# Hashed attention and a gated layer on one core: the loads of the first heads, the bits of the queries, and the place where the first late set's weights are fetched

## The chip, the core and the metric

The kernel runs on one core of a Trainium2 chip. The core has a matrix engine (PE; its weight loads are shown apart, as PEld), a vector engine (DVE), an activation engine (ACT), a general engine (POOL) and a queue engine that only issues transfers (SP). Each executes its instructions in the order in which they were written, and waits on semaphores for the others. Transfers are issued from SP, and a few from ACT; 16 DMA engines carry them out. The metric is the device time of one execution, in microseconds (us).

## What is computed

Four batches of eight heads, 768 tokens each, 64 numbers per head. A key counts for a query only if the signs of six projections agree; the heads' results, laid side by side, go through a gated layer with 1536 inner columns:

```python
q_bits = (np.einsum('bhsd,dk->bhsk', q, proj) > 0).astype(np.int64)
k_bits = (np.einsum('bhsd,dk->bhsk', k, proj) > 0).astype(np.int64)
...
mask = q_bucket[:, :, :, None] == k_bucket[:, :, None, :]
scores = scale * np.matmul(q, k.transpose(0, 1, 3, 2))
scores = np.where(mask, scores, -1000000000.0)
...
attn = np.exp(scores)
attn = attn / (np.sum(attn, axis=-1, keepdims=True) + 1e-09)
return np.matmul(attn, v).astype(np.float32)
...
gate = 1.0 / (1.0 + np.exp(-(x @ w_gate)))
val = x @ w_val
return (gate * val @ w_out).astype(np.float32)
```

## The kernel before

The work is a list of tasks. Each names an engine, a key, an estimated duration, the tasks that it comes after and the buffers that it takes and gives back. A planner (`Plan.order`) walks through the list in estimated time; on each engine the task with the smallest key that is ready and has its buffers goes next. What it writes down is the fixed order of each engine. So an estimate decides an order, but no duration on the chip.

**The heads.** There are 16 pairs of heads. Of each pair the keys and queries are loaded (kr, qr), turned on PE (tk, tq, L945), copied (kx, qx), and split into a high and a low part (kh, kl, qh, ql) whose three cross products make up a full-precision product. SP copies the queries' parts into the other half of the partitions (qsh, qsl, L974). A product with the projection (hs, L980; its table is hw) gives the signs, DVE makes bits of them (L987), and SP spreads these over two tiles, qb (four transfers, L993) and kb (four, L1002). A score task (sc, L1053 and L1059) is one product of the bits, which pushes unlike pairs apart, and six of the parts. DVE finds the extreme and moves the scores to e (L1069), ACT takes the exponential (L1077), PE turns e (tp, L1110), DVE or ACT copies it to ef (L1117), and PE multiplies with the values (pv, L1127; vr is the loaded v). The sums go by two transfers through memory (rd, rb) to POOL, which divides (xs, L1137); SP stores xs to xd. A pair has 12 score tasks, in two groups of six.

At the start, PE runs 60 matmuls on a tile of zeros whose result nobody reads (idle, L271, the fillers). They have the largest key of all.

**The weights.** They come as 64-bit numbers. Beside the heads, DVE, ACT and POOL convert and split them (L320 to L384). The pieces of the first two blocks of 128 inner columns stay on chip; the others go to memory (kg, kv, ko).

**The early units.** A unit is half of a batch's tokens. It loads xd to xr (L463), casts xh on ACT (L470), subtracts xl on POOL or DVE (L474), and does for the first two blocks two gate products (zg, L500), two value products (zv), a gated product gf (DVE, L516) split into gh and gl (L520, L521), and three output products (zo, L533), copied to ob and stored as part.

**The late sets.** After the heads, the other ten blocks are done in five sets of two, batch by batch, each by seven products (z1 to z7, L719) of sums of four blocks of x (a11, a12, a21, a22, s1 to s4). The blocks are loaded as ra (L617); the sum of two of them, s1, stands in a tile that is named sc like the scores (L625). The weights of a set are ten fetches, four wg, four wv, two wo (L688). They begin with the task `switch`, which closes the pools of the heads' stage and opens the late ones.

## Time and profile before

| | us |
|---|---|
| median of 3 runs | 1017.61 |
| lowest and highest | 1016.65, 1025.71 |
| profiled execution | 1016.87 |
| its span in the trace | 1014.9 |
| PE, DVE, ACT, POOL busy | 979.6, 762.2, 559.9, 288.2 |

The span runs from the first to the last instruction in the trace; the execution's own time has another 2 us around it. The heads end at about 513, the last early unit at about 557; the late sets fill the rest. In the profile's rows an instruction stands with its start, its duration and, in brackets, how long its engine sat idle before it and what ended that. An arrow in a wait reads "waited for". A busy share of PE counts the fillers too.

### The profile page before, as it was taken

The numbers are of one execution on the slowest core, as the hardware profiler recorded it, in microseconds if no ns is written. First come the engines' busy times: TensorE is split into PE (matmuls) and PEld (weight loads), VectorE is DVE, ScalarE is ACT, GpSimd is POOL, SyncE is SP. The second block draws the span as 40 slices with busy tenths as digits, with TensorE's granted clock in tenths as the row PEclk, the third lists the DMA queues.
The fourth block names the chain that finished last, engine by engine and source line by source line (L and its number), as shares of the span: only waits on it lengthen the run. The fifth ranks groups of instructions, "written<-read, shape, count | busy, mean of one in ns | idle before, by whom it ended". The sixth has DMA issues, their size and how long they took to land.

```text
span 1014.9 us, 20971 instructions
## 1 busy us (share of the span) xinstructions
PE 979.6 (97%) x8108; PEld 779.9 (77%) x8108; DVE 762.2 (75%) x1412; ACT 559.9 (55%) x1022; POOL 288.2 (28%) x259
## 2 busy tenths in 40 slices
PE   7999999999999999999979999999999999999998
PEld 3665566676666666675668989999989989999897
DVE  2878997898777778887615787888787778787864
ACT  1778787877677778887644352343233325242430
POOL 4024346555554366463443121211000000000000
PEclk9999999999999999999998999999999999999999
DMA  7355666576775668645467977588359671505021
GB/s 159 90 148 147 168 170 176 183 227 180 219 200 190 183 179 261 184 144 184 167 245 261 383 285 258 203 281 310 140 185 385 210 274 42 187 16 171 32 93 63
DMA packets 145988, 192.43 MB, mean 190 GB/s; under 512 B 65248, under 2 KB 104416, under 8 KB 145888
## 3 DMA queue, kind: packets, MB, share of 16 engines
q1 hardware_dynamic: 144160, 190.69, 58.3%
q8 instruction: 64, 1.05, 0.4%
q10 hardware_dynamic: 1728, 0.40, 0.2%
q14 instruction: 36, 0.29, 0.1%
HBM read 127.41 MB, written 49.28 MB: 174 GB/s over the span
## 4 chain that ended last, share of the span: by engine, by line
PE 78%; DVE 8%; DMA 6%; SPq 3%; ACT 2%; issue 1%; POOL 1%; DVEq 0%; ACTq 0%; POOLq 0%
PE yo L838 16%; PE pv L1127 11%; PE sc L1059 7%; PE tp L1110 5%; PE zo L533 3%; DVE e L1069 3%; PE sc L1053 3%; PE zg L500 3%; DMA rawv<-in_moe_w_val_dram 2%; PE zv L500 2%; PE z4g L719 2%; PE z1g L719 2%; PE z1v L719 2%; PE z4v L719 2%; PE z7v L719 2%; PE z3v L719 2%
## 5 line engine op out<-in xcount | busy, mean ns | idle before, releaser
L1077 ACT ACTIVATE e<-e,st 128x768 f32<-128x768 f32 x192 | 178.6, 932 | 47.8 <-DVE e L1069 47.0
L1069 DVE TENSOR_SCALAR_CACHE_REDUCE e<-sc 128x768 f32<-128x768 f32 x192 | 176.3, 953 | 26.9 <-PE sc L1059 26.0
L1127 PE MATMUL pv<-ef,vr 128*64 128x384 f32 x768 | 143.4, 503 | 0.8 <-DVE ef L1117 0.8
L1110 PEld LDWEIGHTS tp<-ident,e 64*128 64x128 f32 x2304 | 84.6, 139 | 36.5 <-issue 14.7
L1110 PE MATMUL tp<-ident,e 64*128 64x64 f32 x2304 | 95.3, 226 | 7.2 <-DVE e L1069 3.1
L1117 DVE COPY ef<-tp 128x768 f32<-128x768 f32 x88 | 83.0, 950 | 21.5 <-PE tp L1110 21.4
L1117 ACT COPY ef<-tp 128x768 f32<-128x768 f32 x104 | 81.3, 797 | 31.1 <-PE tp L1110 30.5
L1127 PEld LDWEIGHTS pv<-ef,vr 128*64 128x64 f32 x768 | 48.8, 138 | 57.8 <-issue 48.7
L1059 PE MATMUL sc<-kh,ql 64*128 64x384 f32 x192 | 89.8, 468 | 0.0
L1059 PE MATMUL sc<-kh,qsl 64*128 64x384 f32 x192 | 89.8, 468 | 0.0
L1053 PE MATMUL sc<-kb,qb 64*128 64x384 bf16 x384 | 66.1, 330 | 10.4 <-DMA kb<-bits 2.7
L1059 PE MATMUL sc<-kh,qh 64*128 64x384 f32 x192 | 64.3, 335 | 0.0
L1059 PE MATMUL sc<-kh,qsh 64*128 64x384 f32 x192 | 64.2, 335 | 0.0
L1059 PE MATMUL sc<-kl,qh 64*128 64x384 f32 x192 | 64.0, 333 | 0.0
L1059 PE MATMUL sc<-kl,qsh 64*128 64x384 f32 x192 | 64.0, 333 | 0.0
L1053 PEld LDWEIGHTS <-qb 64*128 64x128 bf16 x384 | 22.6, 94 | 49.7 <-issue 41.1
L1137 POOL TENSOR_TENSOR xs<-xs,rb 128x384 f32<-128x384 f32 x32 | 32.7, 1022 | 71.4 <-DVE xs L1134 60.4
L739 ACT COPY snm1g<-z1g 128x384 f32<-128x384 f32 x20 | 9.6, 481 | 76.1 <-PE z1g L719 76.1
L838 PE MATMUL yo<-wo,gh 128*128 128x512 f32 x144 | 44.6, 391 | 0.0
L877 DVE TENSOR_TENSOR ol<-yo,ol 128x512 f32<-128x512 f32 x36 | 24.7, 687 | 23.4 <-PE yo L838 22.8
L500 PE MATMUL zg<-xh,wg 128*128 128x384 f32 x128 | 38.7, 361 | 3.6 <-ACT xh L470 3.6
L1059 PEld LDWEIGHTS sc<-kh,qsl 64*128 64x128 f32 x192 | 37.3, 194 | 1.5 <-issue 1.5
(562 smaller groups left out, 2817.7 us busy)
## 6 DMA issues: line engine op xcount, KB each, us to landing
wg<-kg SPq DMA_DIRECT2D x33, 512.0 KB
wv<-kv SPq DMA_DIRECT2D x33, 512.0 KB
ra<-xd SPq DMA_DIRECT2D x32, 384.0 KB
wo<-ko SPq DMA_DIRECT2D x22, 512.0 KB
part<-ob SPq DMA_DIRECT2D x36, 256.0 KB
kg<-pkg SPq DMA_DIRECT2D x15, 512.0 KB
kv<-pkv SPq DMA_DIRECT2D x15, 512.0 KB
kr<-in_k_dram SPq DMA_DIRECT2D x64, 96.0 KB
```

Of the source, the lines that this page charges most:

```text
L500: nc.tensor.matmul(z["acc"][:, :GN], a[:, wc], x[xx][c // 2][:, c % 2, :], start=(c == 0 and i == 0), stop=(c == KC - 1 and i == 2),)
L533: nc.tensor.matmul(acc, a[:, slot, ts_], w, start=(first and i == 0), stop=(last and i == 2))
L719: nc.tensor.matmul(bank[m], a[:, wc], x[xx, block][:, c, :], start=(c == 0 and i == 0), stop=(c == 1 and i == 2),)
L838: nc.tensor.matmul(accs[t], a[:, ts_], w, start=(start and jj == 0 and q == 0), stop=(stop and jj == 1 and q == 2),)
L1053: nc.tensor.matmul(sc[:, j, :GN], z["qb"][rows, c], z["kb"][rows, h], start=True, stop=False, tile_position=(j * D, 0),)
L1059: nc.tensor.matmul(sc[:, j, :GN], q_[rows, c], z["k" + x][rows, h * GN : (h + 1) * GN], start=False, stop=(m == 2), tile_position=(j * D, 0),)
L1069: nc.vector.tensor_scalar(sp(e), gz["sc", t, h][:, :, :GN], MASKED, None, op0=ALU.min, op1=ALU.min, accum_out=gz["st", t][:, h : h + 1],)
L1077: nc.scalar.activation(e, e, AF.Exp, bias=st[:, h : h + 1], scale=-1.0, accum_out=gz["su"][:, h * GT + t : h * GT + t + 1],)
L1110: nc.tensor.transpose(tp[:, r, at_ : at_ + D], gz["e", t, h][rows, c * P : (c + 1) * P], ident[rows, rows], tile_position=(r * D, 0),)
L1117: copy(gz["ef", c].rearrange("p (n r d) -> p r n d", r=2, d=D), gz["tp", c][:, :, :GN].rearrange("p r (n d) -> p r n d", d=D),)
L1127: nc.tensor.matmul(gz["pv"][rows, :GN], z["v"][:, h, c], gz["ef", c][:, h * GN : (h + 1) * GN], start=(c == 0), stop=(c == NC - 1), tile_p ...
L1137: nc.gpsimd.tensor_mul(gz["xs"], gz["xs"], gz["rb"])
```

## The change

**Start.** The zeros of the fillers have a tile of their own, set by POOL before anything else; before, they were the last of POOL's settings. The table hw is cleared on DVE. A small activation at the head of ACT makes the activation table load there. The projection is loaded ahead of the queries, both from ACT. In the plan, the second pair's loads come after the first pair's have landed, the third pair's after all that the first pair needs, and the first values after the first keys and queries. The low parts of the first pair are left to DVE.

**Bits.** The four row groups of hs are arranged otherwise, so that DVE writes the bits of the queries into qb itself: half of the query columns stand where the scores read them, and two transfers, not four, bring the other half across. For the lower partitions the two halves of qb are then swapped (`beyond`). The keys' bits are spread from qb; for the first pair ACT issues these four transfers.

**Weights and the late stage.** The conversion starts at step 6 of the scores, not 12, with two buffers for raw weights in place of one. The staging tiles and kr, qr, kx, qx lie in a pool on the other side of the memory. When the early weights and the last pair's tiles are done with it, a task `first` closes that pool and opens one for the ten weights of the set that is worked first. `switch` then waits until the last stores of xs have begun, not ended, and the new pools wait tile by tile. The ra loads get a larger key, and a12 is split second. The fetches of the second set wait for the early product that last used their tile, not for the last of all. The planner no longer chooses a filler because its tiling fits.

At the start, SP before and now, from the first row (kr, qr, vr with the pair in the number; the size behind):

```order
L928 DMA kr_0_218<-in_k_dram 128x3x64 x4
L937 DMA vr_0_227<-in_v_dram 128x2x384
L928 DMA kr_1_230<-in_k_dram 128x3x64 x4
L933 DMA qr_1_243<-in_q_dram 128x6x64 x2
L937 DMA vr_1_251<-in_v_dram 128x2x384
L928 DMA kr_2_287<-in_k_dram 128x3x64 x4
L974 DMA qsh_0_311<-qh_0_302 64x768 x2
L933 DMA qr_2_321<-in_q_dram 128x6x64 x2
L993 DMA qb_198<-bits_0_338 24x384 x4
L974 DMA qsl_0_367<-ql_0_303 64x768 x2
L1002 DMA kb_200<-bits_0_338 12x384 x4
```

```order
L941 DMA kr_0_225<-in_k_dram 128x3x64 x4
L950 DMA vr_0_262<-in_v_dram 128x2x384
L941 DMA kr_1_277<-in_k_dram 128x3x64 x4
L946 DMA qr_1_302<-in_q_dram 128x6x64 x2
L987 DMA qsh_0_312<-qh_0_294 64x768 x2
L1004 DMA qb_207<-qb_207 24x384 x2
L987 DMA qsl_0_332<-ql_0_295 64x768 x2
L950 DMA vr_1_351<-in_v_dram 128x2x384
L987 DMA qsh_1_388<-qh_1_380 64x768 x2
```

The keys' spread (kb) of the first pair and the queries' load of the third are gone from here, the queries' spread is halved, and the third pair's keys stand behind the swapped queries. ACT at the same place, before and now (hw is the projection's table, warm the small activation):

```order
L933 DMA qr_0_215<-in_q_dram 128x6x64 x2
L241 DMA hw<-in_proj_dram 64x6 x2
L961 ACT_TABLE_LOAD
L961 ACTIVATE kx_0_285<-tk_0_259 128x2x6x64
L965 CAST kh_0_297<-kx_0_285 128x768
L961 ACTIVATE kx_1_395<-tk_1_325 128x2x6x64
L965 CAST kh_1_400<-kx_1_395 128x768
L1077 ACTIVATE e_0_0_0_0_440,su_177<-e_0_0_0_0_440,st_0_0_0_439 128x768
```

```order
L231 ACT_TABLE_LOAD
L231 ACTIVATE warm<-warm 128x1
L260 DMA hw<-in_proj_dram 64x6 x2
L946 DMA qr_0_230<-in_q_dram 128x6x64 x2
L974 ACTIVATE kx_0_282<-tk_0_249 128x2x6x64
L978 CAST kh_0_289<-kx_0_282 128x768
L1011 DMA kb_209<-qb_207 12x384 x4
L974 ACTIVATE kx_1_353<-tk_1_337 128x2x6x64
L978 CAST kh_1_369<-kx_1_353 128x768
```

The table load and the projection stand ahead of the queries, and kb's four transfers ahead of the second pair's copy. On PE the fillers before stood 21 ahead of the first turns, 12 behind them and 27 behind the second pair's turns; now 15 stand ahead, 5 behind, 17 before the second pair's turns, 2, 5 and 3 around those and its hash, and 13 among the first scores and turns: 1, 1, 8, 1, 1 and 1.

At the end of the heads, SP before, from the last sums on (ko is the last converted weight, ra and xr the late and the early loads of xd):

```order
L1091 DMA rd_97<-sv_3_1_8384 4x32x32
L317 DMA rawo_8444<-in_moe_w_out_dram 128x1024
L1098 DMA rb_3_1_8451<-rd_97 64x384 x2
L384 DMA ko_108<-pko_108_8457 128x1024
L1140 DMA xd_65<-xs_3_0_8483 128x384
L463 DMA xr_0_8551<-xd_65 128x2x384
L463 DMA xr_0_8552<-xd_65 128x2x384
L384 DMA ko_109<-pko_109_8594 128x1024
L1140 DMA xd_65<-xs_3_1_8616 128x384
L590 DMA part_100<-ob_2_1_8632 128x512
L590 DMA part_100<-ob_2_1_8646 128x512
L590 DMA part_100<-ob_2_1_8658 128x512
```

and now, from the same transfer (rd_97) on:

```order
L1113 DMA rd_97<-sv_3_1_8360 4x32x32
L700 DMA wg_4_00_8403<-kg_0_116 128x1024
L1120 DMA rb_3_1_8409<-rd_97 64x384 x2
L700 DMA wg_4_00_8415<-kg_1_117 128x1024
L700 DMA wg_4_00_8431<-kg_2_118 128x1024
L700 DMA wg_4_00_8461<-kg_3_119 128x512
L700 DMA wv_4_00_8471<-kv_0_136 128x1024
L700 DMA wv_4_00_8476<-kv_1_137 128x1024
L700 DMA wv_4_00_8481<-kv_2_138 128x1024
L700 DMA wv_4_00_8486<-kv_3_139 128x512
L700 DMA wo_4_00_8494<-ko_104 128x1024
L700 DMA wo_4_00_8497<-ko_105 128x1024
```

All ten fetches stand before the store of the last pair's first half (xd, then part and xr, follow directly); before, the first fetch was the eighth row behind those shown here. PE around the last values product (pv_3_1), before:

```order
L1127 MATMUL pv_3_1_8537<-ef_3_1_5_8589,vr_3_7825 64x384 x2
L533 MATMUL zo_2_1_8612<-wo_2314,gl 128x512
L533 MATMUL zo_2_1_8612<-wo_2314,gh 128x512 x2
L533 MATMUL zo_2_1_8612<-wo_2669,gl 128x512
L533 MATMUL zo_2_1_8612<-wo_2669,gh 128x512 x2
L533 MATMUL zo_2_1_8622<-wo_2314,gl 128x512
L533 MATMUL zo_2_1_8622<-wo_2314,gh 128x512 x2
L533 MATMUL zo_2_1_8622<-wo_2669,gl 128x512
L533 MATMUL zo_2_1_8622<-wo_2669,gh 128x512 x2
```

and now:

```order
L1149 MATMUL pv_3_1_8556<-ef_3_1_4_8598,vr_3_7849 64x384 x2
L1149 MATMUL pv_3_1_8556<-ef_3_1_5_8604,vr_3_7849 64x384 x2
L544 MATMUL zo_2_1_8616<-wo_1897,gl 128x512
L544 MATMUL zo_2_1_8616<-wo_1897,gh 128x512 x2
L544 MATMUL zo_2_1_8616<-wo_2118,gl 128x512
L544 MATMUL zo_2_1_8616<-wo_2118,gh 128x512 x2
L511 MATMUL zg_3_0_8660<-xh_0_8646,wg_1071 128x384
L511 MATMUL zg_3_0_8660<-xl_0_8648,wg_1071 128x384
L511 MATMUL zg_3_0_8660<-xh_0_8646,wg_1071 128x384 x2
```

Before, a third zo followed. One output product of the unit 2_1 is left behind the last pv, two have moved ahead of it. DVE in the same place (sc is the sum s1), before:

```order
L516 TENSOR_TENSOR gf_2_1_8607<-zv_2_1_8585,sig 128x384
L633 TENSOR_TENSOR a11l_0_8740<-ra_0_8683,a11h_0_8727 128x768
L516 TENSOR_TENSOR gf_3_0_8747<-zv_3_0_8712,sig 128x384
L625 TENSOR_TENSOR sc_0_8754<-ra_0_8685,ra_0_8705 128x768
L516 TENSOR_TENSOR gf_3_0_8777<-zv_3_0_8736,sig 128x384
L633 TENSOR_TENSOR s1l_0_8812<-sc_0_8754,s1h_0_8768 128x768
```

and now:

```order
L1139 COPY ef_3_1_5_8604<-tp_3_1_5_8585 128x2x6x64
L645 TENSOR_TENSOR a11l_0_8694<-ra_0_8651,a11h_0_8680 128x768
L637 TENSOR_TENSOR sc_0_8704<-ra_0_8658,ra_0_8666 128x768
L645 TENSOR_TENSOR a12l_0_8719<-ra_0_8655,a12h_0_8699 128x768
L637 TENSOR_TENSOR ra_0_8658<-ra_0_8651,ra_0_8658 128x768
L527 TENSOR_TENSOR gf_3_0_8734<-zv_3_0_8709,sig 128x384
L645 TENSOR_TENSOR s1l_0_8739<-sc_0_8704,s1h_0_8721 128x768
L527 TENSOR_TENSOR gf_3_0_8770<-zv_3_0_8730,sig 128x384
```

The first gf of the unit 3_0 has moved behind three operations on ra.

The core of the diff:

```diff
+    mp = ctx.enter_context(tc.tile_pool(name="moe", bufs=1))
+    xp = ctx.enter_context(tc.tile_pool(name="xp", bufs=1))
+    w1 = ctx.enter_context(tc.tile_pool(name="w1", bufs=1))
+    ph1 = ExitStack()
+    ph0 = ExitStack()
+    stage1 = ph0.enter_context(tc.tile_pool(name="stage1", bufs=1, side="right"))
+    at = ph1.enter_context(tc.tile_pool(name="attn", bufs=2))
+    zero = stage1.tile([P, 512], BF16, name="zero")
+    nc.gpsimd.memset(zero, 0.0)
+    warm = const.tile([P, 1], F32, name="warm")
+    nc.vector.memset(warm, 0.0)
+    nc.scalar.activation(warm, warm, AF.Exp)
...
+        for at_ in (m * HB, m * HB + D):
+            rows = slice(at_, at_ + HB)
+            nc.vector.tensor_add(thr[rows], picked[rows, :1], picked[rows, 1:])
+            nc.vector.memset(mul[rows], 1.0 if m else APART)
...
     sig = mp.tile([P, J1, GN], F32, name="sig")
-    zero = sig[:, 0].bitcast(BF16)[:, :512]
     idle = ps.tile([P, 512], F32, name="idle", tag="one")
-    nc.gpsimd.memset(zero, 0.0)
...
-    W_KEY, W_STEP = 12.0, 2.2
+    W_KEY, W_STEP = 6.0, 2.2
-        ef=4, qx=1, kx=1, raw1=1, cv1=1, wk1=2, raw2=1, cv2=1, wk2=1, xr=1, x=1, ob=3, ol=3, sn=4, sg=6, gf=4, sc=1, port=1,
+        ef=4, qx=1, kx=1, raw1=2, cv1=1, wk1=2, raw2=1, cv2=1, wk2=1, xr=1, x=1, ob=3, ol=3, sn=4, sg=6, gf=4, sc=1, port=1,
...
-                FIRST, 393216, lambda: load(name), after=stored[b, int(name[1]) - 1] + [later["switch"]], take=[f"r{name}"],
+                FIRST + 0.5, 393216, lambda: load(name), after=stored[b, int(name[1]) - 1] + [later["switch"]], take=[f"r{name}"],
...
-        for name in ("a11", "a21", "a22", "a12"):
+        for name in ("a11", "a12", "a21", "a22"):
             raw(name)
         ready = z["ready"]
         pieces_of("a11")
+        pieces_of("a12")
-        pieces_of("a12")
...
-                to = later["x"].tile([P, 2, size], F32R, name=f"w{n}{m}_{js[0]}_{at_[0]}{at_[1]}", tag=f"w{slot}{n}{m}")
+                to = later["x" if slot else "p"].tile([P, 2, size], F32R, name=f"w{n}{m}_{js[0]}_{at_[0]}{at_[1]}", tag=f"w{slot}{n}{m}")
...
-            after=[made_piece[key_], later["switch"], last_fetch.get(role)] + after, take=[role],
+            after=[made_piece[key_], later["switch" if slot else "first"], last_fetch.get(role)] + after, take=[role],
...
-                at_ = slice(m % 2 * GN, (m % 2 + 1) * GN)
+                at_ = slice(m // 2 * GN, (m // 2 + 1) * GN)
                 nc.tensor.matmul(
-                    z["hs"][m * HB : (m + 1) * HB, 0, :GN], hw["w"], z["qx" if m < 2 else "kx"][:, at_],
+                    z["hs"][m * HB : (m + 1) * HB, 0, :GN], hw["w"], z["kx" if m % 2 else "qx"][:, at_],
...
-            z["bits"] = at.tile([P, GN], BF16, name=f"bits{u}", tag="bits")
-            nc.vector.tensor_scalar(z["bits"], z["hs"][:, 0, :GN], thr, mul, op0=ALU.is_gt, op1=ALU.mult)
+            z["qb"] = qbs[i % 2]
+            nc.vector.tensor_scalar(z["qb"][:, :GN], z["hs"][:, 0, :GN], thr, mul, op0=ALU.is_gt, op1=ALU.mult)
 
         def spread_q():
-            z["qb"] = qbs[i % 2]
             for j in range(2):
-                for m in range(2):
-                    nc.sync.dma_start(
-                        z["qb"][j * D : j * D + HW, m * GN : (m + 1) * GN], z["bits"][m * HB : m * HB + HW],
-                    )
-
-        def spread_k():
+                nc.sync.dma_start(z["qb"][j * D : j * D + HW, GN:], z["qb"][(1 - j) * D : (1 - j) * D + HW, :GN])
+
+        def spread_k(eng):
             z["kb"] = kbs[i % 2]
             for j in range(2):
                 for h in range(2):
-                    at_ = D + h * HB + j * HS
-                    nc.sync.dma_start(z["kb"][j * D + h * HS : j * D + (h + 1) * HS, h], z["bits"][at_ : at_ + HS])
-
+                    at_ = h * D + HB + j * HS
+                    eng.dma_start(z["kb"][j * D + h * HS : j * D + (h + 1) * HS, h], z["qb"][at_ : at_ + HS, :GN])
...
+        if i == 0:
+            hw["loaded"] = add(t0 - 11, "act", 1200, load_projection)
+            hw["landed"] = add(0, "pool", 0, lambda: None, after=[hw["loaded"], add(0, "pool", 4000, lambda: None)])
         here = {
             n: add(t0 - 10.72, "act" if i == 0 and n == "q" else "sp", 1200 if n == "q" else 2400,
-                   lambda n=n: load(n, nc.scalar if i == 0 and n == "q" else nc.sync), tail=4000, take=[n + "r"])
+                   lambda n=n: load(n, nc.scalar if i == 0 and n == "q" else nc.sync), tail=4000, take=[n + "r"],
+                   after=(first_loads[:2] if i == 1 else first_loads if i == 2 else []) + [last_loads.get(n)] + [hw["loaded"]] * (i == 0 and n == "q"))
...
         if i == 0:
-            a = add(t0 - 10, "act", 1200, load_projection, after=[], tail=2500)
-            hw["task"] = add(t0 - 10, "dve", 1500, hash_weights, after=[a])
+            first_loads.extend(here.values())
+        last_loads.update(here)
+        if i == 0:
+            hw["task"] = add(t0 - 10, "dve", 400, hash_weights, after=[hw["landed"]])
...
-        for fn in (spread_q, spread_k):
-            needs.append(add(t0 - 2.6, "sp", 2400, fn, after=[bits_], tail=2500))
+        needs.append(add(t0 - 2.6, "sp", 1200, spread_q, after=[bits_], tail=2500))
+        if i == 0:
+            needs.append(add(t0 - 2.6, "act", 2400, lambda: spread_k(nc.scalar), after=[bits_], tail=2500))
+        else:
+            needs.append(add(t0 - 2.6, "sp", 2400, lambda: spread_k(nc.sync), after=[bits_], tail=2500))
...
-        v_here = dma(t0 - 5, 393216, load_v, take=["vr"])
+        if i == 0:
+            first_loads.extend(needs)
+        v_here = dma(t0 - 5, 393216, load_v, take=["vr"], after=first_loads[:2] + [last_loads.get("v")])
+        last_loads["v"] = v_here
...
+            c, beyond = (slice((m * GT + t) * P, (m * GT + t + 1) * P) for m in (g, 1 - g))
...
-                    sc[:, j, :GN], z["qb"][rows, c], z["kb"][rows, h], start=True, stop=False, tile_position=(j * D, 0),
+                    sc[:, j, :GN], z["qb"][rows, beyond if j else c], z["kb"][rows, h], start=True, stop=False, tile_position=(j * D, 0),
...
+    def first_switch():
+        ph0.close()
+        later["p"] = ctx.enter_context(tc.tile_pool(name="latep", bufs=1, side="right", reuse_waits="tile"))
+
+    later["first"] = add(0, "sp", 0, first_switch, after=early_kept + heads_done)
...
         for n in "xtw":
-            later[n] = ctx.enter_context(tc.tile_pool(name=f"late{n}", bufs=1))
-        later["ps"] = ctx.enter_context(tc.tile_pool(name="ps3", bufs=6, space=PSUM))
-
-    later["switch"] = add(0, "sp", 0, switch, after=every + early_kept, give=["moe"] * 2)
+            later[n] = ctx.enter_context(tc.tile_pool(name=f"late{n}", bufs=1, reuse_waits="tile"))
+        later["ps"] = ctx.enter_context(tc.tile_pool(name="ps3", bufs=6, space=PSUM, reuse_waits="tile"))
+
+    later["switch"] = add(0, "sp", 0, switch, after=[later["first"]], begun=every, give=["moe"] * 2)
...
-                        fetch_piece((i, b), js, slot, n, m, [last_early] if (i, b) == (0, 0) and slot == 1 else [], (i, b) == (0, 0))
+                        first = (i, b) == (0, 0) and slot == 1
+                        free = last_g if (n, m) in (("g", 0), ("g", 1)) else last_x if (n, m) in (("g", 2), ("v", 0)) else last_early
+                        fetch_piece((i, b), js, slot, n, m, [free] if first else [], first)
```

## What was predicted before the run

> **What bounds the kernel now.** I read the engine totals first (PE busy 97% of the span), then the busy time by stretches, then who PE waited for, then the instructions in order of time around the two waits that the change touches. Positions are microseconds from the start of the span. In the late stretches PE is busy all of the time; it has holes at the start and where the heads give way to the late sets:
>
> ```profile
> 512.80:525.80 13.00, 12.97 (x68) 11.56 (x66) 1.43 (x2) 6.18 (x12) 5.80 (x6) 1.00 0.65 224
> 525.80:541.00 15.20, 9.09 (x24) 6.10 (x25) 5.86 (x5) 4.54 (x9) 7.83 (x6) 0.66 0.95 361
> 541.00:567.40 26.40, 26.40 (x146) 25.37 (x146) 17.83 (x28) 12.90 (x24) 5.25 (x4) 1.00 0.79 273
> ```
>
> The columns are the stretch, its length, then busy time and instructions of PE, PEld, DVE, ACT and POOL, the granted clock, the DMA share and GB/s. From 525.8 to 541.0 PE runs 24 matmuls, at a granted clock of 0.66, while DMA is 95% busy: this stretch is set by transfers. The waits of PE:
>
> ```profile
> PE idle L271 <- POOL sig L268: 4.8, 1, 4.8
> PE zg L500 <- ACT xh L470: 3.6, 1, 3.6
> ...
> PE sc L1053 <- DMA kb<-bits: 2.7, 3, 1.3
> ```
>
> The first and (mostly) the third lie at the start, the second at the change of stage. The page's busy share of PE hides the start: the 60 matmuls on idle count as busy there.
>
> **The start.** Its rows, by engine:
>
> ```profile
> 4.21 0.53 POOL L268 MEMSET sig<- 128x512 bf16 x1
> ...
> 4.79 0.13 PEld L271 LDWEIGHTS <-sig 128*128 128x128 bf16 x2 [4.79 <-POOL sig L268]
> ...
> 10.74 1.22 PEld L271 LDWEIGHTS <-sig 128*128 128x128 bf16 x6 [0.28 <-issue]
> ...
> 12.38 0.59 PE L945 MATMUL tk<-ident,kr 64*128 64x64 f32 x12
> 12.80 0.54 PE L945 MATMUL tq<-ident,qr 64*128 64x64 f32 x12
> 13.28 2.76 PE L271 MATMUL idle<-sig 128*128 128x512 bf16 x12
> 15.97 0.52 PE L980 MATMUL hs<-qx,hw 128*32 128x384 f32 x2
> ...
> 26.20 0.32 PE L1053 MATMUL sc<-kb,qb 64*128 64x384 bf16 x1 [0.54 <-DMA kb<-bits]
> ```
> ```profile
> 6.31 1.60 ACTq L241 DMA_DIRECT2D hw<-in_proj_dram  x2
> 7.94 1.28 ACT L961 ACT_TABLE_LOAD   x1 [7.94 <-DMA vr<-in_v_dram]
> ```
> ```profile
> 10.46 0.17 DVE L246 TENSOR_SCALAR hw<-hw 64x6 f32<-64x6 f32 x1 [7.91 <-DMA hw<-in_proj_dram]
> ...
> 13.38 0.96 DVE L957 TENSOR_SCALAR qx<-tq 128x768 f32<-128x768 f32 x1 [2.03 <-PE tq L945]
> ...
> 16.89 0.68 DVE L987 TENSOR_SCALAR bits<-hs,thr,mul 128x384 bf16<-128x384 f32 x1 [1.96 <-PE hs L980]
> ```
> ```profile
> 17.76 3.55 SPq L993 DMA_DIRECT2D qb<-bits  x4
> 21.42 1.17 SPq L974 DMA_DIRECT2D qsl<-ql  x2
> 22.63 3.11 SPq L1002 DMA_DIRECT2D kb<-bits  x4
> ```
>
> Fourteen fillers stand 0.425 us apart (4.79 to 10.74), the later ones 0.23 (2.76/12). The first scores reach their pace at 26.1 (the second matmul starts at 26.20), because SP issues 4 + 2 + 4 transfers after the bits, 17.76 to 25.74.
>
> After the change, step by step. The zeros are POOL's first work: 0.73 + 0.53, so PE starts at 1.3, not 4.79. It has 15 fillers ahead of the keys' turn, not 21: 14 x 0.425 + 0.23 = 6.2, so the keys' turn starts at 7.6 and the queries' could at 8.0. The queries' load now stands on ACT behind the table load (1.28), a tiny activation (about 0.2) and the two projection loads (1.60): issued from about 3.9 to 5.3. Nothing shows its landing alone; the nearest row is the projection's, issued at 6.31 and used at 10.46, 4.15. The lower end is 2.7 (PE then never waits), the upper 5.3 + 4.15 = 9.4; I take 8.3, nearer to the end at which few transfers compete. The table load costs nothing, it runs ahead of any data, as before. From the queries' turn the chain is: 0.58 to the copy (12.80 to 13.38), 0.96, and 0.1 to the hash: 9.95. The hash takes 0.8, 17 fillers 3.9, the second pair's turns with 2 fillers between them 1.4, its query copy 0.1 + 0.96 + 0.2, its hash 0.8, 3 fillers 0.7, and gaps of 0.3: first scores at 19.1, say 19.3. The other branch is shorter: bits at 11.4 (the low keys now stand ahead of them on DVE), 0.68, four issues on ACT at 0.78 (3.11/4), and 0.5 to land (25.74 to 26.20): 15.7. On SP two issues of 0.89 (3.55/4) and the swapped low queries (1.17) end at 15.1. So the wait on the bits' transfers is gone, and PE's own order (fillers, second pair) is late next. Gain 26.1 - 19.3 = 6.8, ends 5.7 and 7.4.
>
> It is partly given back: 13 fillers now stand among the first scores, 13 x 0.23 = 3.0. But in that stretch the chain of work that ended last runs on DVE, and PE has holes:
>
> ```profile
> 27.08 4.57 DVE e L1069 x11
> ```
> ```profile
> 35.35 0.28 PE L1110 MATMUL tp<-ident,e 64*128 64x64 f32 x2 [0.48 <-ACT e L1077]
> ...
> 37.39 0.34 PE L1053 MATMUL sc<-kb,qb 64*128 64x384 bf16 x2 [0.72 <-DVE ef L1117]
> ```
>
> Two of the fillers stand among the first ten scores, under DVE's pace, 0.5; the holes hide 1.2. So 1.3 is lost (ends 0 and 3.0).
>
> **The heads.** The queries' spread falls from 4 issues to 2 in each of 16 pairs, 1.8 us of SP time each; PE waited on these transfers once outside the start, 1.3 at most. Gain between 0 and 1.3, I take 0.5. The weights' conversion starts 6 steps sooner with the same number of operations: 0, with an end of 2 each way, since it reshuffles who waits. DVE now writes the bits into the tile that the scores read; the pair that read it last is a whole pair back, so nothing queues behind that: 0.
>
> **The change of stage.** Its rows:
>
> ```profile
> 511.32 1.51 PE L1127 MATMUL pv<-ef,vr 128*64 128x384 f32 x8
> ...
> 531.47 0.69 PE L500 MATMUL zg<-xh,wg 128*128 128x384 f32 x1 [3.61 <-ACT xh L470]
> ```
> ```profile
> 543.60 2.08 PE zg L500 x12
> ...
> 553.68 3.44 PE zo L533 x15
> ```
> ```profile
> 517.48 0.59 ACT L577 COPY ob<-zo 128x512 f32<-128x512 f32 x1 [0.36 <-PE zo L533]
> ...
> 522.93 0.84 ACT L629 CAST a11h<-ra 128x768 fp32r<-128x768 f32 x1 [0.78 <-DMA ra<-xd]
> ...
> 530.18 0.83 ACT L629 CAST a12h<-ra 128x768 fp32r<-128x768 f32 x1 [4.40 <-DMA ra<-xd]
> ```
> ```profile
> 513.65 1.00 POOL L1137 TENSOR_TENSOR xs<-xs,rb 128x384 f32<-128x384 f32 x1
> ...
> 515.83 2.96 POOL L474 TENSOR_TENSOR xl<-xr,xh 128x384 fp32r<-128x384 f32 x3 [0.19 <-ACT xh L470]
> ```
> ```profile
> 529.20 0.96 DVE L625 TENSOR_TENSOR sc<-ra,ra 128x768 f32<-128x768 f32 x1 [3.97 <-DMA ra<-xd]
> ```
> ```profile
> 497.83 1.10 SPq L1098 DMA_DIRECT2D rb<-rd  x2
> ```
> ```profile
> 518.59 1.99 SPq L617 DMA_DIRECT2D ra<-xd  x2
> ...
> 521.65 0.98 SPq L617 DMA_DIRECT2D ra<-xd  x2
> ...
> 523.31 4.04 SPq L688 DMA_DIRECT2D wg<-kg  x4
> ```
>
> Loss now: from 525.8 to 541.0 PE does 12 zg and 12 zo matmuls, at full pace 2.08 + 12 x 3.44/15 = 4.8, in 15.2: 10.4 lost. On ACT, xh stands behind a12h, which waits for ra until 530.18, and DVE waits for ra until 529.20; these loads share DMA with the fetches issued from 523.31.
>
> With the change the ten fetches (eight of 512 KB, two of 256 KB, 4.72 MB) stand ahead of the last unit's loads. At the 361 GB/s of the stretch above they take 13.1 us, from about 499 (the rb issues end at 498.93) to 512. This is covered by the last heads' transposes and products, up to about 513; without that cover it would all be PE idle. The ra loads then compete only with one raw weight and xr.
>
> New waits. Let T be the end of the last values product (512.8 before). Two of the three zo stand before it now, so only 1.4 of PE work lies between T and the next unit's zg. That needs xl, four on POOL in a row at 0.99 (2.96/3), behind the division (1.00) and behind the ACT copy of the last ob: POOL is free of xs at T + 1.9 (513.65 + 1.00), the third zo ends at T + 1.4, its copy at T + 2.1 (0.59), xh at T + 2.6, xl runs from T + 2.7 to 6.7, zg ends at T + 7.2, against T + 3.5 unhindered: 3.7 lost. Next, DVE has its sc (needs two ra), a12l and another before gf, gf before zo. Each ra lands 4.3 (518.59 to a11h at 522.93) to 7.6 us (521.65 to 529.20, the fetches beside it) after its issue. Issued from T + 3.3 to T + 5, the last lands between T + 9.3 and T + 12.6; at T + 12 zo waits 1.5. Sum of new waits 5.2, ends 1.5 (xl hidden) and 10.4 (nothing won). Gain 10.4 - 5.2 = 5.2, ends 0 and 8.9.
>
> The granted clock was 0.66 after 5.7 us with about 1 us of matmuls (525.8 to 531.5). At zg PE will have 2.1 of matmuls in 5.8, and no row shows whether that keeps the clock. A clock as slow as that of the first fillers, for as long (5.95), would cost 3.0, and the result would be 1009.4; I take none, since each hole is under 1 us. The Trainium skill ("TensorE: Matmul & The Clock Gate", Part 1: The HAM clock gate) has a rule that speaks against any new wait of this kind: the clock is halved after an idle window of about 3.4 us and restored after a busy one. By that rule a window with a third of its time in matmuls is not idle, and 1006.4 stands; counted as idle it would give the 1009.4. The trace agrees with the halving, but its first fillers stayed slow longer than one window.
>
> **Sum.** 6.8 - 1.3 + 0.5 + 5.2 = 11.2. The profiled execution took 1016.87 (span 1014.9), so 1005.7; the median of the runs shown is 0.74 above it: 1006.4.
>
> **Rivals.** (a) Only the start is won: DVE and ACT still stand behind ra, and xl paces zg, so the change of stage costs 10.4 as before: 1017.6 - 6.0 = 1011.6. For it: ra at the head of both in-order engines, as at 529.20 and 530.18, and all four ra ahead of the last xr on SP now; against: 4.72 MB less competes with them. (b) The new waits are only 1.5: 1017.6 - 6.0 - 8.9 = 1002.7; it needs xl early, and POOL's rows speak against that. (c) Slower: the ten fetches crowd the last heads, and xr of the next to last unit, behind them on SP, comes late.
>
> ```profile
> DMA packets 145988, 192.43 MB, mean 190 GB/s; under 512 B 65248, under 2 KB 104416, under 8 KB 145888
> ```
>
> At the mean of the span they take 24.8, from 499 to 524, and xr lands at about 527 instead of 514: 12.6 of idle PE, 5.2 of the waits above and up to 3 of slow clock, 20.8 in place of 10.4; less the 6.0 of the start, 1022.0. It decides from xr after 525, a rate under some 200 GB/s; the 361 speaks against it. (d) The change does not do what it says: in the order the first pair's values stand directly behind its keys on SP with no wait, and the second pair's keys wait only for an earlier transfer. If the queries' turn came no sooner than now (12.8), the first scores would stand at 23.8: 4.5 less, 1010.9. Against it: the first pair's keys and queries were in before 12.4 even now, with both pairs' loads and the values side by side.
>
> **How the numbers follow.** About 1% (1007.4 and 1027.8) is what a measurement of this kernel can tell from no change. Forecast 0.55 (its own range 1002.5 to 1010; 0.36 of it below 1007.4, 0.19 above); (a) 0.17 and (d) 0.07, within 1%; (b) 0.14, faster; (c) 0.07, of it 0.04 beyond 1027.8. That makes faster 0.36 + 0.14 = 0.50, within 1% 0.19 + 0.17 + 0.07 + 0.03 = 0.46, slower 0.04. The range 1000.5 to 1013 leaves out (c) and about 0.1 at the edges of the others.
>
> **What would show it.** PE's first filler at 1.3 and the first scores at about 19 with no wait for the bits' transfers: the start holds. Ten fetches landed before the last values product, and DMA clearly under 95% in the 15 us after it: the cover holds. PE waiting at zg for xl on POOL, about 3.7 in pieces under 1 us, and then at zo or z2g for what DVE does behind ra: the new waits hold. The forecast is wrong if the first scores stand after 22, if PE loses more than 10 between the last values product and the second late set, or if the heads themselves take over 3 us more or less than the 486.7 that lie between 26.1 and 512.8 now.

## The result and the profile after

| | median us | runs | ratio to before, 95% interval |
|---|---|---|---|
| before | 1016.37 | 12 | |
| changed | 1009.81 | 12 | 0.9932 [0.9909, 0.9955] |

The change gains 6.6 us, 0.7%: faster, but within the 1% that was called hard to tell from no change. The profiled execution took 1009.79 (before 1016.87), a gain of 7.1. The changed kernel's engines, busy in its span of 1008.0 us:

```profile
PE 982.1 (97%) x8108; PEld 781.1 (77%) x8108; DVE 763.1 (76%) x1415; ACT 560.9 (56%) x1028; POOL 283.4 (28%) x256
```

PE is still the engine that is always busy. Who PE waited for, in the changed kernel (total, times, longest):

```profile
PE z6g L731 <- ACT snm1g L751: 4.7, 1, 4.7
...
PE zg L511 <- POOL xl L485: 1.5, 4, 0.6
PE zo L544 <- POOL gl L532: 1.5, 1, 1.5
...
PE zg L511 <- ACT xh L481: 1.1, 1, 1.1
```

Of the waits that the change was to remove, none is left: no 4.8 at the first filler, no wait for the bits at the start, no 3.6 at zg. But the longest wait is a new one, in the late sets, where PE's order is that of before.

**The start.** Its rows in order of time:

```profile
1.31 5.60 PE L282 MATMUL idle<-zero 128*128 128x512 bf16 x15 [1.31 <-POOL zero L228]
...
6.84 0.59 PE L958 MATMUL tk<-ident,kr 64*128 64x64 f32 x12
...
9.08 0.59 PE L958 MATMUL tq<-ident,qr 64*128 64x64 f32 x12 [1.65 <-DMA qr<-in_q_dram]
...
11.57 3.84 PE L282 MATMUL idle<-zero 128*128 128x512 bf16 x17
...
16.40 0.59 PE L958 MATMUL tq<-ident,qr 64*128 64x64 f32 x12
...
19.64 0.80 PE L1075 MATMUL sc<-kb,qb 64*128 64x384 bf16 x2
```

The first scores stand at 19.64 (26.1 before), and what precedes them is PE's own order: fillers, the second pair's turns, its hash. This start has a slower variant: in two of the twelve profiles that have it (e7 and e10 below) PE waits 1.85 and 2.10 for qr, not 1.65, the five fillers behind the turn take 2.3 and not 1.25, and the first scores stand at 21.8 and 21.6.

**The change of stage.** The last values product ends at 502.5. The stretches from there on, columns as in the prediction (length; busy time and instructions of PE, PEld, DVE, ACT, POOL; clock, DMA share, GB/s):

```profile
490.00:502.50 12.50, 12.50 (x114) 7.46 (x112) 2.47 (x3) 4.60 (x8) 1.97 (x2) 1.00 0.90 341
502.50:512.50 10.00, 8.10 (x30) 6.39 (x31) 0.96 (x1) 4.76 (x9) 4.90 (x5) 0.83 0.99 318
512.50:518.00 5.50, 5.50 (x34) 5.50 (x33) 2.52 (x3) 1.41 (x3) 0.00 (x0) 1.00 0.82 287
518.00:530.00 12.00, 9.66 (x43) 7.08 (x42) 7.97 (x11) 7.51 (x15) 7.39 (x6) 1.00 0.22 80
530.00:543.80 13.80, 13.75 (x73) 12.64 (x72) 8.63 (x15) 6.11 (x12) 4.70 (x4) 1.00 0.88 312
```

The stretch with DMA at 0.95 and clock 0.66 of before is gone. PE loses time in two places now, 502.5 to 512.5 and 518 to 530, and in the second DMA is mostly idle (0.22). In order of time:

```profile
505.16 0.44 PE L511 MATMUL zg<-xh,wg 128*128 128x384 f32 x1 [1.09 <-ACT xh L481]
505.19 3.89 POOL L485 TENSOR_TENSOR xl<-xr,xh 128x384 fp32r<-128x384 f32 x4 [1.03 <-ACT xh L481]
...
512.52 0.33 PE L511 MATMUL zv<-xh,wv 128*128 128x384 f32 x1
...
515.48 0.96 DVE L637 TENSOR_TENSOR sc<-ra,ra 128x768 f32<-128x768 f32 x1 [4.28 <-DMA ra<-xd]
...
520.42 0.50 PE L544 MATMUL zo<-wo,gl 128*128 128x512 f32 x1 [1.45 <-POOL gl L532]
```

In the first of the two the granted clock falls at 507.5, behind 3.4 us in which PE ran six matmuls:

```profile
504.10:507.50 3.40, 1.52 (x6) 0.95 (x7) 0.00 (x0) 2.23 (x5) 2.37 (x4) 1.00 0.97 337
507.50:510.90 3.40, 3.40 (x12) 2.87 (x11) 0.66 (x1) 1.29 (x2) 1.58 (x2) 0.51 1.03 343
```

**The lead along the kernel.** To see where time goes when PE is "busy" throughout, I took the same matmul in both traces (in the late sets both orders are the same from z4g on, so the n-th low-part matmul of a kind is the same one) and subtracted its start in the changed kernel from its start in before. Four of them, before and then changed:

```profile
559.24 0.33 PE L719 MATMUL z4g<-a22l,wg 128*128 128x384 f32 x1
...
639.02 0.33 PE L719 MATMUL z2g<-a12l,wg 128*128 128x384 f32 x1
...
644.58 0.33 PE L719 MATMUL z7g<-s3l,wg 128*128 128x384 f32 x1
...
994.30 0.33 PE L719 MATMUL z4v<-a22l,wv 128*128 128x384 f32 x1
```
```profile
543.99 0.34 PE L731 MATMUL z4g<-a22l,wg 128*128 128x384 f32 x1
...
622.07 0.34 PE L731 MATMUL z2g<-a12l,wg 128*128 128x384 f32 x1
...
634.03 0.34 PE L731 MATMUL z7g<-s3l,wg 128*128 128x384 f32 x1
...
987.12 0.34 PE L731 MATMUL z4v<-a22l,wv 128*128 128x384 f32 x1
```

The lead is 15.25, 16.95, 10.55 and 7.18 us. In the heads, where work was moved, I compare the copies xs of the heads' results and add the work that stands ahead of one of them in one kernel only, at full pace; at the last head that is 512.88 - 502.58 = 10.3 and 12 zo products more already done (12 x 0.228 = 2.7).

| stretch | predicted gain | measured gain | lead after it |
|---|---|---|---|
| start | 6.8 | 6.5 | 6.5 |
| fillers among the scores, and heads | -0.8 | +6.5 | 13.0 |
| last head to z4g of the first late set | 5.2 | 2.2 | 15.2 |
| to 622 | 0 | 1.7 | 16.9 |
| 622 to 634 | 0 | -6.4 | 10.5 |
| 634 to the end | 0 | -3.4 | 7.2 |
| sum | 11.2 | 7.2 | |

So the kernel was once 17 us ahead and gave back almost 10, in stretches where neither the order of PE nor the amount of work differs from before. First the six microseconds, in the changed kernel:

```profile
605.00:615.00 10.00, 10.00 (x58) 9.77 (x57) 5.14 (x9) 2.64 (x6) 4.39 (x6) 1.00 1.01 374
615.00:624.00 9.00, 9.00 (x53) 8.85 (x51) 5.80 (x11) 2.21 (x5) 0.47 (x1) 1.00 1.03 406
624.00:634.00 10.00, 5.27 (x17) 5.10 (x17) 5.12 (x11) 3.84 (x8) 1.49 (x2) 0.66 0.58 232
```
```profile
619.65 0.32 SPq L395 DMA_DIRECT2D kv<-pkv  x1
...
627.44 0.62 ACT L385 CAST pkv<-t12v 128x512 fp32r<-128x512 f32 x1 [8.44 <-DMA kv<-pkv]
...
628.39 0.46 ACT L751 COPY snm1g<-z1g 128x384 f32<-128x384 f32 x1
...
628.90 0.69 PE L731 MATMUL z6g<-s2h,wg 128*128 128x384 f32 x1 [4.73 <-ACT snm1g L751]
```

The late packed weights have one buffer (wk2). Its write-back is issued at 619.65 and lands 7.8 later, beside fetches that keep DMA full (1.03, 406 GB/s). ACT's next cast waits for it, and behind the cast stand the copies that free PE's result banks. PE stops 4.73, and its clock is 0.66 in the ten microseconds around. The Trainium skill ("Perfetto Trace Analysis", Tensor Engine Instruction (MATMUL, LD_WEIGHTS)) says that ACT, DVE and GpSimd work strictly in order; the trace agrees, the copy starts 0.95 after the cast though its data had been there for six microseconds.

The other 3.4 has no wait at all. Two stretches of the changed kernel, with weights of another set and with weights that lie where the ten early fetches put theirs:

```profile
691.62 0.33 PE L731 MATMUL z5v<-s1h,wv 128*128 128x384 f32 x1
...
692.66 0.33 PE L731 MATMUL z6v<-s2h,wv 128*128 128x384 f32 x1
```
```profile
706.36 0.34 PE L731 MATMUL z5v<-s1h,wv 128*128 128x384 f32 x1
...
707.42 0.34 PE L731 MATMUL z6v<-s2h,wv 128*128 128x384 f32 x1
```

The same six matmuls on the same inputs take 1.04 and 1.06. In the whole late part the groups (the six matmuls of one product) of sets 4 and 10, whose weights share the early pool (slot 0), take 1.06 and the others 1.04; before, and with the start alone (below), all take 1.04. The output products (yo) show it too, more strongly. Six of them from the first row to the second, with wo of set 4, and six from the third to the fourth, with wo of set 6 (the number behind the bracket):

```profile
738.65 0.40 PE L850 MATMUL yo<-wo,gl(0, 1)4_0_2_10769 128*128 128x512 f32 x1
...
740.06 0.39 PE L850 MATMUL yo<-wo,gl(0, 1)4_0_2_10769 128*128 128x512 f32 x1
...
746.97 0.39 PE L850 MATMUL yo<-wo,gl(0, 1)6_0_2_10999 128*128 128x512 f32 x1
...
748.33 0.39 PE L850 MATMUL yo<-wo,gl(0, 1)6_0_2_10999 128*128 128x512 f32 x1
```

1.41 against 1.36. The late part has 672 matmuls of z and 288 of yo on that pool, so each kind costs about 2 us (0.003 and 0.0065 apiece); part of it falls ahead of 634.

### The profile page after: what moved, and what is told of

Read it like the earlier page. It is cut to its first block, busy times and chain, and to the rows that moved or that the text cites. A ratio compares the mean times of both kernels' runs of the same rounds, so it can differ in the third digit from the quotient of the medians.

```text
span 1008.0 us, 20931 instructions
## 1 busy us (share of the span) xinstructions
PE 982.1 (97%) x8108; PEld 781.1 (77%) x8108; DVE 763.1 (76%) x1415; ACT 560.9 (56%) x1028; POOL 283.4 (28%) x256
## 3 DMA queue, kind: packets, MB, share of 16 engines
q8 instruction: 64, 1.05, 0.4%
## 4 chain that ended last, share of the span: by engine, by line
PE 80%; DVE 6%; DMA 4%; ACT 4%; issue 2%; POOL 2%; SPq 1%; ACTq 0%; DVEq 0%; POOLq 0%
PE yo L850 16%; PE pv L1149 11%; PE sc L1081 7%; PE tp L1132 6%; PE zo L544 3%; PE sc L1075 3%; PE zv L511 3%; DVE e L1091 3%; PE z6g L731 2%; PE zg L511 2%; PE z7g L731 2%; PE z1v L731 2%; PE z6v L731 2%; PE z7v L731 2%; PE z4g L731 2%
## 5 line engine op out<-in xcount | busy, mean ns | idle before, releaser
L1149 PE MATMUL pv<-ef,vr 128*64 128x384 f32 x768 | 140.4, 496 | 0.0
L1081 PEld LDWEIGHTS sc<-kh,ql 64*128 64x128 f32 x192 | 37.2, 194 | 1.2 <-POOL wo L388 0.8
```

What stands on the lines that cost most here:

```text
L1081: nc.tensor.matmul(sc[:, j, :GN], q_[rows, c], z["k" + x][rows, h * GN : (h + 1) * GN], start=False, stop=(m == 2), tile_position=(j * D, 0),)
L1149: nc.tensor.matmul(gz["pv"][rows, :GN], z["v"][:, h, c], gz["ef", c][:, h * GN : (h + 1) * GN], start=(c == 0), stop=(c == NC - 1), tile_p ...
```

## The experiments

Ratios are against runs of before on the same chip; several chips were used.

| run | median us | runs | ratio, 95% interval |
|---|---|---|---|
| e1 casts later | 1003.33 | 6 | 0.9868 [0.9840, 0.9896] |
| e2 start alone | 1001.75 | 6 | 0.9849 [0.9820, 0.9877] |
| e3 conversions sooner | 1021.64 | 12 | 1.0045 [1.0020, 1.0070] |
| e4 fetch at the switch | 1010.88 | 11 | 0.9941 [0.9918, 0.9963] |
| e5 weights moved by 32 bytes | 1002.61 | 4 | 0.9856 [0.9831, 0.9882] |
| e6 fewer fillers | 1001.06 | 5 | 0.9840 [0.9814, 0.9865] |
| e7 low parts on DVE | 998.24 | 5 | 0.9813 [0.9789, 0.9837] |
| e8 other set moved | 1003.64 | 4 | 0.9863 [0.9838, 0.9888] |
| e9 same remainder | 998.95 | 5 | 0.9832 [0.9812, 0.9853] |
| e10 start, second raw buffer | 1000.32 | 4 | 0.9848 [0.9834, 0.9861] |
| e11 e9 with one raw buffer | 1002.17 | 4 | 0.9866 [0.9852, 0.9880] |
| e12 e9, e6 and e7 together | 993.92 | 4 | 0.9783 [0.9766, 0.9799] |

**e1: ACT's late casts put later.**

```diff
-        return low_, dma(key, 1024 * size, lambda: nc.sync.dma_start(to, f(z["w"])), after=[low_], give=[wk])
+        return low_, dma(key, 1024 * size * (5 if late else 1), lambda: nc.sync.dma_start(to, f(z["w"])), after=[low_], give=[wk])
```

> The changed kernel, with one number of the planner altered: for the late write-backs of packed weights it now reckons five times the transfer time, so it puts ScalarE's late casts (pkg, pkv, pko) later on that engine; TensorE's order is the same, matmul for matmul. In the changed kernel TensorE stands 4.7 us at 624.2 for a copy on ScalarE, which stands behind the cast of a packed weight, which waits 8.4 us for the write-back that still holds its buffer; with slow matmuls after it the lead over the kernel before falls from 16.9 to 10.6 there. Theory A (position): the copies stand behind the wrong instruction; with the casts later TensorE has no wait over 1 us between 600 and 660, and the time is 1009.8 - 6 = 1003 to 1005. Theory B (transfers): the 16 queues are full there (1.00 to 1.04, 372 to 406 GB/s from 605 to 625), TensorE has only run ahead of what they can feed it, and will wait for a weight instead: 1008 to 1011.

1003.33: 6.5 less than the changed kernel, by one number in the planner's picture of a transfer. Position it was; DMA is as full as in the changed kernel, and PE has no hole and the full clock:

```profile
615.00:624.00 9.00, 9.00 (x53) 9.00 (x53) 8.05 (x17) 3.97 (x9) 0.00 (x0) 1.00 1.05 399
624.00:634.00 10.00, 10.00 (x59) 10.00 (x58) 6.81 (x14) 4.11 (x9) 2.36 (x3) 1.00 0.51 196
```

The transfers do not bound PE there.

**e2: the start alone**, on the conversions, the fetch and the late order of before (from the changed kernel, undone):

```diff
-    W_KEY, W_STEP = 6.0, 2.2
+    W_KEY, W_STEP = 12.0, 2.2
...
-        ef=4, qx=1, kx=1, raw1=2, cv1=1, wk1=2, raw2=1, cv2=1, wk2=1, xr=1, x=1, ob=3, ol=3, sn=4, sg=6, gf=4, sc=1, port=1,
+        ef=4, qx=1, kx=1, raw1=1, cv1=1, wk1=2, raw2=1, cv2=1, wk2=1, xr=1, x=1, ob=3, ol=3, sn=4, sg=6, gf=4, sc=1, port=1,
...
-        for name in ("a11", "a12", "a21", "a22"):
+        for name in ("a11", "a21", "a22", "a12"):
...
-    later["first"] = add(0, "sp", 0, first_switch, after=early_kept + heads_done)
```

> The kernel before with the start part alone (zeros first, table and projection first, first loads alone, bits written in place, first keys' bits spread from ScalarE); conversion times, the fetch and the change of stage are those of before. First scores at 19.6 as in the changed kernel, against 26.1. If the prediction's term holds (6.5 less about 1 for the fillers among the scores): 1016.4 - 5.5 = 1011, and the lead over before, cleared of moved work, is 5 to 6 at the first head and stays so to the last. Rival: the start also causes what the heads won beyond that (7.5 more between the first head and the last): 1004. Rival: the lead is lost again at the change of stage, where transfers rule: 1015 to 1017.

1001.75: none of the three, and 8 less than the whole change. The lead is 5.7 at the first head, as priced, 9.4 at the last, 13.1 at the end; no cast stops PE, and all groups take 1.04. From the last head to z4g, where e2's code is that of before, it gains 1.8 all the same, nearly the 2.2 of the whole change. The rest of the change, taken together, costs time; cleared of the two losses of the late sets it is about even (e9, below: 998.95, and ratios whose intervals overlap).

**e3: only the conversions sooner**, on before.

```diff
-    W_KEY, W_STEP = 12.0, 2.2
+    W_KEY, W_STEP = 6.0, 2.2
```

> The kernel before with one number altered: the first weights' conversions are due 6 steps sooner (12 to 6). The prediction put this at 0, with 2 either way. Rival: the heads' unforeseen gain (7.5 between the first head and the last) is this number's doing, because other instructions then stand in front of the exponentials: last values product 6 to 8 sooner and, if nothing is lost behind it, 1009 to 1010.

4.6 slower, outside the 2 that the prediction allowed; the lead over before is -4.0 at the last head. The rival, that this number alone made the heads' gain, falls.

**e4: the ten fetches back at the switch.**

```diff
-            after=[made_piece[key_], later["switch" if slot else "first"], last_fetch.get(role)] + after, take=[role],
+            after=[made_piece[key_], later["switch"], last_fetch.get(role)] + after, take=[role],
```

> The changed kernel, except that the ten weights of the first late set are fetched at the switch again, as before; the pools, the order of the late inputs and all else stay. By the prediction the early fetch keeps 24 matmuls from a stretch where transfers rule: without it TensorE loses 10 or more between the last values product and the second late set, in place of 8.8, so 1011.5 to 1015. Rival: the tail gives the lead back anyway (it fell from 16.9 to 10.6 at 624), so a later arrival there costs nothing: 1009 to 1010.5.

1010.88 against 1009.81, the intervals overlap; from last head to z4g the gain over before is 1.8 (11.1 to 12.9) in place of 2.2. So the early fetch itself is worth 1 or less. What e4 keeps and before lacks is the rest of the new stage: a12 split second, the other pools, and the ra loads sooner, 3.0 to 5.0 behind the last head's copy (504.54; before 5.7 to 9.8) and with no xr among them. Ahead of the fetches they stand in both:

```profile
507.54 1.98 SPq L629 DMA_DIRECT2D ra<-xd  x4
509.57 1.03 SPq L700 DMA_DIRECT2D wg<-kg  x2
```

**e5 and e9: the early-fetched weights at other addresses**, on e1. A pad behind them in their pool, 32 bytes in e5 and 160 in e9 (40 in place of 8 below):

```diff
+            if (n, m) == ("o", 1) and not slot and "pad" not in later:
+                later["pad"] = later["p"].tile([P, 8], F32, name="pad", tag="pad")
```

> The kernel of the run with later casts, and 32 bytes more at the end of the pool of the first late set's weights, which moves these weights from addresses 32 above a multiple of 64 to multiples of 64, where the late inputs and the other set's weights lie; no order changes. In the changed kernel six matmuls take 1.06 where the weights come from that pool (wg_4, wv_4, wg_10, wv_10) and 1.04 with the other weights, the late inputs being the same, and the lead over before falls from 10.6 to 7.2 between 634 and 987. Theory A (address within 64 bytes, unlike that of the late input): 1.04 everywhere, no fall, 1003.3 - 3.3 = 1000. Theory B (the place on the right side of the memory, or the clock of that run): the groups stay at 1.06 and the time at 1003.3.

> The kernel with later casts, and 160 bytes behind the first late set's weights in place of 32, so that their addresses have the same remainder modulo 256 (64) as the late inputs and the other set's weights; no order changes. In the runs so far six matmuls took 1.04 where weights and inputs had the same remainder modulo 256 (before: 32 and 32; start alone: 64 and 64) and 1.05 to 1.06 where they differed by 32 to 160 (changed kernel 224 against 64; with 32 bytes 192 against 64; the run with the pool w1 moved 96 against 128). Theory A (remainder): 1.04 everywhere, the lead over before falls by less than 1 between 634 and 987 in place of 2.8 to 3.4, time 1002.6 - 2.8 = 999.8. Theory B (the place: the last pool on the right): still 1.05 to 1.06 and 1002 to 1003.

e5: still 1.05 to 1.06, the lead falls by 2.8 and not 3.4; the rule of 64 bytes falls. e9: 1.04 in every group, and the lead stays at 17.8 from 643 of before to the end. Six matmuls on weights in the early pool in e9:

```profile
695.40 0.33 PE L733 MATMUL z4g<-a22h,wg 128*128 128x384 f32 x1
...
696.44 0.33 PE L733 MATMUL z1v<-a11h,wv 128*128 128x384 f32 x1
```

Against e1 the time falls by 4.4 (1003.33 to 998.95; ratios 0.9868 and 0.9832, whose intervals overlap, while the trace shows 3.4).

**e8: the other set's weights moved**, on e2 (whose groups all take 1.04), 32 bytes ahead of the pool w1 and 32 behind it.

```diff
+    w1.tile([P, 8], F32, name="pad0")
...
+        w1.tile([P, 8], F32, name="pad1")
```

> The start-alone kernel with 32 bytes put ahead of the weights pool w1 and 32 behind it, so that the other late set's weights (wg, wv pieces 0 to 2 of sets 2, 6 and 8) lie 32 above a multiple of 64 while the late inputs and the first set's weights stay at multiples of 64. Orders may change a little with the pools, so the groups are what counts. Theory A (address): now wg_2, wv_2, wg_6, wv_6, wg_8, wv_8 take 1.06 for six matmuls and wg_4, wv_4, wg_10, wv_10 take 1.04; about 860 matmuls by 0.0035 is 3.0 slower than start alone. Theory B (place or clock): all at 1.04, as with start alone, 1001.8.

In sets 2, 6 and 8 the groups with inputs at remainder 128 take 1.05 to 1.07, those of 4 and 10 take 1.04 (1.05 in some): the slow set changes with the address and not with the place. But the input counts as well. With weights at 96, the groups on s1 (at 128) are slow and most of those on a22 and s3 (at 64) are not:

```profile
679.47 0.34 PE L732 MATMUL z5g<-s1h,wg 128*128 128x384 f32 x1
...
680.53 0.34 PE L732 MATMUL z6g<-s2h,wg 128*128 128x384 f32 x1
...
683.68 0.34 PE L732 MATMUL z4g<-a22h,wg 128*128 128x384 f32 x1
...
684.72 0.34 PE L732 MATMUL z1v<-a11h,wv 128*128 128x384 f32 x1
```

The time is 1.9 above e2 where 3.0 was expected, and the intervals overlap; in the trace the lead over before falls by 2.1 from 643 to the end, and e2's by 0.3. Start addresses in the built kernels, modulo 256:

```
kernel       slot 0 weights   other weights   inputs (a11, a12, s1, s2 / s4, s3, a22)   slow groups
before             32               32              32 / 32                            none
changed           224               64              64 / 64                            slot 0
e5                192               64              64 / 64                            slot 0
e9                 64               64              64 / 64                            none
e8                128               96             128 / 64                            the others, on inputs at 128
```

(Pieces 3 of the other weights, which z3 uses, lie at 128 in e8.)

**e6: 47 fillers**, on e5.

```diff
-    WARM, FILL = 8, 60
+    WARM, FILL = 8, 47
```

> The kernel with later casts and aligned weights, with 47 idle matmuls in place of 60, so that none stands among the first scores. The prediction put these 13 at a loss of 1.3 (0 to 3.0). By that term the time falls by 1.3 against the run without this edit, to 998.7. Rival: the planner's order in the heads comes out otherwise after it, and that moves the time by more than the fillers, 4 either way (as conversions due sooner did, 4.6 slower).

1.6 less by medians (1002.61 to 1001.06, intervals overlap), 2.8 less in the traces at the last head. Both lie in the term's 0 to 3.0, but they are not the fillers alone. At the first head's copy, behind twelve of the 13, e6 is only 0.23 ahead of e5 (41.47 and 41.70), and after it the orders of DVE and ACT in the heads come out otherwise. The fillers themselves cost some tenths; the rival, the planner's other order, is not excluded for the rest.

**e7: the low parts of the very last unit on DVE**, on e5.

```diff
-                [("pool", 960, lambda c=c: low(c, nc.gpsimd)), ("dve", 470, lambda c=c: low(c, nc.vector))],
+                [("dve", 470, lambda c=c: low(c, nc.vector))] if b == B - 1 and g == NG - 1 else
+                [("pool", 960, lambda c=c: low(c, nc.gpsimd)), ("dve", 470, lambda c=c: low(c, nc.vector))],
```

> The kernel with later casts and aligned weights, where the low parts xl of the very last unit are computed on VectorE alone (0.47 planned) and not on GpSimd (four in a row at 0.97). In the changed kernel the 24 zg matmuls of that unit take from 505.16 to 512.52, 7.4 for 4.2 of work. If xl paces them, as the prediction had it (3.7): zg done 2 to 3 sooner and the time 2 to 2.5 shorter than the run without this edit, 997.5 to 998. Rival: the next wait takes it over (zo behind GpSimd's gl, behind VectorE, which waits for ra until 515.5): zg is shorter, zo waits longer, the time is the same within 1.

The expectation gave the wrong rows: the zg from 505 to 512 belongs to the unit before the last, which keeps its POOL work; the edit acts after 518. There it works: from last head to z4g the trace of e7 has 37.7 (506.96 to 544.66) and that of e5 39.9 (503.52 to 543.42). The same stretch, e5 and then e7:

```profile
518.00:531.00 13.00, 12.15 (x58) 9.65 (x57) 8.93 (x12) 8.21 (x16) 7.41 (x6) 1.00 0.22 74
```
```profile
522.00:535.00 13.00, 12.91 (x67) 11.57 (x67) 9.25 (x15) 8.95 (x18) 4.06 (x4) 1.00 0.45 137
```

67 matmuls in place of 58, with 3.4 less on POOL. So POOL, which did gl and xl in turn, paced 518 to 530. The pair e9 and e12 repeats it: 40.1 and 37.4 from last head to z4g. By medians e7 is 4.4 below e5, twice the expected 2 to 2.5; the intervals just overlap, and nothing in the two traces accounts for more than the 2.2.

**e10 and e11: the second buffer for raw weights**, added to e2 and taken from e9.

```diff
-        ef=4, qx=1, kx=1, raw1=1, ...
+        ef=4, qx=1, kx=1, raw1=2, ...
```

> The start-alone kernel with a second buffer for the raw weights (raw1 2 in place of 1); conversions keep their due times. VectorE waited for raw weights 8.6 in the heads of before and 10.1 with the start alone, and 1.2 to 1.9 in the runs with the second buffer. Theory A (the second raw buffer is what the heads won beyond the start's lead): these waits fall under 3 and the time falls from 1001.8 to 998 or 999. Theory B (only the planner's other order): the waits fall, and the time moves by up to 4 either way without a tie to them.

> The kernel of e9 with one buffer for the raw weights in place of two; all else as there. Theory A (second raw buffer carries the heads' gain): VectorE waits 8 or more for raw weights, the lead over before at the last head, cleared of moved work, is 6 to 8 in place of 12, and the time is 4 to 5 longer than e9. Theory B (planner's order only): within 2 of e9, or off it in a way the waits for raw weights do not explain.

The lead at the last head is 14.2 with two buffers and 9.4 with one (e10, e2), 11.3 and 7.5 (e9, e11). The times move less: 1.4 between e2 and e10, their ratios equal (0.9849, 0.9848); 3.2 between e9 and e11, at the edge of what the intervals tell. And the waits for raw weights do not follow: in the heads of before they are

```profile
DVE exg L329 <- DMA rawg<-in_moe_w_gate_dram: 4.4, 2, 3.9
DVE exv L329 <- DMA rawv<-in_moe_w_val_dram: 4.2, 4, 2.4
```

and in e11, which has one buffer too, 2.3, 0.9 and 0.5; in e10, with two, they are still 5.1, where under 3 was expected. Counted from the first scores to the last head, the pairs differ by 7.1 (e2, e10) and 3.6 (e9, e11, the moved work counted), and six profiles of one order by up to 2.2 (next section). So the buffer, or the order that the planner makes with it, carries part of the heads' gain; that it does so by these waits is not shown.

**e12: e9 with 47 fillers and the last low parts on DVE.** Its edits are those of e9, e6 and e7.

> The kernel of e9 with the two edits that gained: 47 idle matmuls, and the low parts of the last unit on VectorE. If the terms add (e6 1.6 by medians and up to 3.0 by its trace, e7 2.2 by the change of stage and 4.4 by medians): e9 less 4 to 6, some 995; if they share the same slack, e9 less 2.

993.92, 5.0 below e9 and 2.2% below before (0.9783 [0.9766, 0.9799]): by medians the terms add, and this is the fastest version. The profiled pair shows 3.1 (0.5 up to the last head, 2.6 from there to z4g).

## Why the prediction was right and where it was wrong

The time lies in the stated range, 3.4 above the forecast (1006.4), and the chances put 0.46 on a change within 1% and 0.50 on a larger gain. That the sum came near is luck in part: errors of both signs cancelled.

- **Start, 6.8: right.** 6.5 measured; fillers from 1.31, the queries' turn at 9.08 inside 8.0 to 9.4, PE's own order last. e2 is 5.7 ahead at the first head once fillers are counted. In two of twelve profiles the gain is 2 smaller (above).
- **Fillers, 1.3: inside its ends, nearer the lower one.** At the first head, where they have passed, taking the 13 away is worth 0.2 (e6 against e5) and 0.6 (e12 against e9).
- **Heads, +0.5 with 2 either way: the range was mis-sized.** From first scores to last values product the changed kernel takes 482.9, not 486.7, with 5.7 more work in it. "Conversions sooner: 0" was a term that moved the time by 4.6 by itself (e3), in the other direction; the second raw buffer was not priced at all, and takes part (e10, e11). Besides, six profiles of kernels with the same order up to there (changed, e1, e4, e5, e7, e9) reach the last head between 502.6 and 507.0; half of that is e7's late start, and from the first scores on they differ by 2.2, which is what one profile can tell of the heads. How the unforeseen 7 divide between buffer, planner's order and spread stays open.
- **Change of stage, 5.2: the mechanism of the new waits was right, one was left out, and the reason for the gain was wrong.** Predicted: 3.7 at zg behind POOL's xl, then 1.5 at zo behind DVE behind ra. Measured: zg from 505.16 to 512.52 for 4.2 of work, and 1.09 ahead of it, 4.3; zo 1.45. The clock, taken as full, was 0.83 in these ten microseconds, so the waits were paid in slow matmuls too: 0.51 from 507.5 to 510.9, 1.7 at most, part of it beneath the wait for xl. The Trainium skill ("TensorE: Matmul & The Clock Gate", Part 1: The HAM clock gate) has the clock halved after an idle window of about 3.4 us. The prediction took a window with a third of its time in matmuls as not idle; the trace speaks against this reading: the longest wait is 1.09, and the 3.4 us ahead of the drop hold six matmuls, 1.0 of work at full pace. That the 1009.4 given for a clock cost of 3.0 lies near the time is chance. Left out was the last unit: POOL's gl and xl in turn, 2.2 by e7, most of the 3.1 that remain of a loss of 8.9 (41.4 from last head to z4g, for 32.5 of work). And the early fetch did not bring the gain (e4). The sooner loads may have, which was not tried by itself; but e2 gains 1.8 there without any of the new stage, so it is not shown that the new stage brought the 2.2 at all. DMA was not under 95% after the last head either (0.99 for ten microseconds), with ra, xr and raw weights.
- **Late sets, 0: the step that failed.** The prediction stopped its sum at the change of stage and took a lead won there as a gain at the end. There it was lost twice: 6.4 to a cast that the planner had placed for a transfer faster than the real one (e1), and 3.4 to weights whose new pool lies at another remainder of the address (e9), in the products z and yo alike. The two together, 9.8 in the trace, answer to 10.9 by medians from the changed kernel to e9 (1009.81 to 998.95).
- **Rivals.** (d), 1010.9, came nearest in time, but its condition did not occur: the queries' turn stands at 9.08, not 12.8. (a), only the start is won, is near too (1011.6) but not in kind: the change of stage was not as costly as before. The slower rival's mechanism did not occur: the fetches were issued from 483 to 490.6, and DMA moved 341 GB/s behind them (490 to 502.5).

## What to carry to other kernels

A lead is a gain only where the last instruction is reached: follow the same matmul through both traces to the end, and look behind the edit for in-order engines whose next instruction waits for a transfer, since the work behind it was placed for the old timing. When an edit adds a pool or changes the size of one, look at the start addresses of the matmul operands; a pad of 160 bytes was worth 3.4 us here. Try parts of a change alone: here the first part was worth more than the whole. And where an edit goes through a planner, ask whether the orders behind it stayed the same, before its gain is put down to the edit.

## What was not expected of the hardware

Matmuls of 128x128 by 384 in fp32r, back to back, took 0.1733 us each where weights and moving input started at the same remainder modulo 256, and 0.1767 (1.9% more) with weights at 224 and inputs at 64, with no wait shown and a granted clock of 1.00. It is the pair that counts, not one address: in e8 weights at 96 took 0.1766 in the mean with inputs at 128 and 0.1741 with inputs at 64, and weights at 128 ran at the fast pace with both. In e5, 192 and 64 took 0.176. The output products, 128x128 by 512, took 0.2276 in the changed kernel with both operands at 64 and 0.2340 (2.8% more) with the moving input, wo, at 224. So an equal remainder was fast in every run, a difference was slow in some pairs and not in others, and what the rule is these runs do not tell.
